# Reordered first loads, an identity load on ScalarE's queue, and eleven products of zeros ahead of the first fold

## The chip, the cores and the metric

The kernel runs on one core of a Trainium2 chip. A core has TensorE (PE: matrix products; the load of the stationary operand is listed apart as PEld), VectorE (DVE), ScalarE (ACT), GpSimd (POOL) and SyncE (SP). SP computes nothing here; it issues transfers between the chip's memory (HBM) and the core's working memory (SBUF). ScalarE and GpSimd can issue transfers too. Products land in PSUM, from which VectorE and ScalarE read. The metric is the time of one execution in device microseconds, as the median of several runs.

## The reference

The input x has 2048 rows of 512 numbers. Each row is normalized (`xn`, mean 0, variance 1), and two branches follow:

```python
xn = layernorm(x)
q, k, v = split(xn @ wqkv)                 # 32 heads of 16 numbers
pq, pk = q @ w_phi[h], k @ w_phi[h]        # a 16x16 matrix for each head
phi = concat(softmax(p), softmax(-p))      # of pq and of pk
o = phi_q (phi_k^T v) / (phi_q phi_k^T 1)  # linear attention
s = o @ wo
h = relu(xn @ W_gate) * (xn @ W_up)        # 1376 hidden numbers
g = silu(h @ W_down)
out = x + s * g
```

All inputs and the output are float32.

## The kernel before, in words

Rows of x are worked on in 16 tiles of 128 rows. Where a product needs more than one pass of reduced precision allows, each operand is split into a high part (a copy in the type float32r, by ScalarE) and a low part (the remainder, by VectorE or GpSimd); `mm3` then makes three products, low by high, high by low and high by high, in that order for each of the four slices of the contraction. So a product by a weight needs the weight's high and low part in SBUF.

The key and query weights aren't used as they come. `fold` (line 226) multiplies each block of 128x128 of a weight's row block with a block-diagonal matrix that holds `w_phi` (`bd_sb`, tile name cb), in plain float32, so that `xn` times the folded weight gives pq or pk at once. A fold of one row block `k` takes four float32 products into one PSUM tile, pfold; each of them stands in the trace as two matmul instructions. Calling what `fold` returns splits the result into the high and low part (wkh, wkl for the key rows, wqh, wql for the query rows). The key weight has four row blocks (`wk_raw[:, k, :]`, tile name wkT); "key row k" is short for row block k here, 128 partitions of 512 numbers, 256 KB.

A tile of x is normalized by `norm_vector` and `norm_vector_apply` (statistics on VectorE, a power on GpSimd, the scaling on VectorE). `turn` (line 304) transposes it on TensorE with the help of an identity matrix (`ident`, four instructions into the tile pxT) and writes the high part of the transposed tile into the tile XT (ScalarE); `lo_xt` (line 300) writes the low part (VectorE). `project` (line 346) multiplies the transposed tile with a weight by `mm3`: pk with the key weight, pv with the value weight, pq with the query weight.

The prologue (from line 829) issues all first loads on SP's queue, in the order in which the lines stand: x tile 0, the constants `bd_sb`, key row 0, the identity, key rows 1 to 3, x tile 1, query rows 0 and 1, value rows 0 and 1, query rows 2 and 3, x tile 2, value rows 2 and 3, x tiles 3 to 6. Then (from line 854) the work is written out by hand: statistics of tile 0; folds of key rows 0 and 1; scaling of tile 0; split of row 0; `turn(0)`; split of row 1; folds of key rows 2 and 3; `lo_xt` of tile 0; split of row 2; statistics of tile 1; split of row 3; scaling of tile 1; then pk of tile 0. The splits of the value rows (`wv_split`, GpSimd for the low part), the folds of the query rows and further tiles follow.

The main loop (line 904) goes over the 16 tiles of x; after it come two halves, each over the 22 blocks of the gate, up and down weights, with the attention's queries and the output between them. Every engine executes its instructions in the order in which the program emits them. `InOrder` and `Clock` (a planner) decide during emission where the pieces of secondary work go: `Clock.issued` charges every instruction with a cost in its own units, keeps for each engine the time at which it is reckoned free, takes a load as ready 8,000 units after its issue, and `due` lets a piece in when its engine is reckoned free soon enough. Its clock `now` is the time at which TensorE is reckoned free. A matmul on float32 operands is charged with

```python
if name == "matmul" and a[2].dtype == F32:
    cost = n * 3 + 460
```

where n is the number of columns. Tiles of SBUF come from pools: `u2` has 44 buffers of 2 KB in each partition, and `ps` is the pool of the eight PSUM tiles.

## Time and profile before

| what | value |
|---|---|
| runs shown, median (lowest to highest) | 586.2 us (585.45 to 586.35) |
| the profiled execution: its time, its span | 586.47 us, 584.7 us |
| PE, PEld busy | 572.5 us (98% of the span), 478.0 us (82%) |
| DVE, ACT, POOL busy | 395.4, 288.6, 390.2 us |
| mean transfer rate over the span | 236 GB/s |
| first product on PE | at 7.06 us |

The profile is one execution of the program, recorded by the hardware. Times in it count from the start of the span. A row of the timeline has the start, the length, the engine, the line (a helper records every operation, so all have line 52), the operation, the tiles written and read, and in brackets the idle time of the engine just before with what ended it. Rows with x16 stand for sixteen instructions in a run, and the matmuls are pipelined, so the last one's drain reaches into the next row. The granted clock is the share of full speed that the throttle of TensorE granted.

### The profile page before, as it was taken

Reading aid. Unit: us, or ns where it says so; the run is one execution under the profiler, and the core shown is the slowest. Engines: PE = TensorE matmul, PEld = TensorE weight load, DVE = VectorE, ACT = ScalarE, POOL = GpSimd, SP = SyncE. Lnnn points to the kernel's source line nnn. Section 1 sums busy time; section 2 is a strip of 40 time slices with the busy share of each in tenths; the row PEclk is TensorE's granted clock in tenths of the full one; section 3 lists DMA queues with packets and bytes.
Section 4 is the critical chain, followed back from the end, with each engine's and each line's share of the span. In section 5 each row is a group of like instructions: output and inputs, shape, how many; then the busy total and the mean of one; then the engine's idle time right before and its main releaser. Section 6 shows DMA issues by size and latency. Waiting matters only on the chain.

```text
span 584.7 us, 8483 instructions
## 1 busy us (share of the span) xinstructions
PE 572.5 (98%) x2764; PEld 478.0 (82%) x2764; DVE 395.4 (68%) x604; ACT 288.6 (49%) x529; POOL 390.2 (67%) x341
## 2 busy tenths in 40 slices
PE   4999999999999999999999999999999999999997
PEld 4788888888888888888888888888888888888886
DVE  2898765876647976787784532488788868673323
ACT  3798786864635356245434151153554545534510
POOL 0669987998866576997967342544457585775394
PEclk9999999999999999999999999999999999999999
DMA  8358897974698938978967999995576475669863
GB/s 289 112 150 223 221 307 233 265 222 126 164 279 272 347 95 261 301 263 293 283 215 226 319 389 398 315 390 193 130 266 170 137 227 169 183 206 275 254 176 113
DMA packets 82844, 138.26 MB, mean 236 GB/s; under 512 B 7664, under 2 KB 30576, under 8 KB 81904
## 3 DMA queue, kind: packets, MB, share of 16 engines
q1 hardware_dynamic: 79488, 125.66, 64.3%
q0 software_dynamic: 3312, 12.06, 10.8%
q8 instruction: 22, 0.36, 0.3%
q14 instruction: 22, 0.18, 0.1%
HBM read 77.14 MB, written 52.69 MB: 222 GB/s over the span
## 4 chain that ended last, share of the span: by engine, by line
PE 97%; DMA 1%; ACT 1%; DVE 1%; SPq 0%; issue 0%; POOL 0%; POOLq 0%
PE py L52 21%; PE pd L52 10%; PE pa L52 10%; PE pc L52 10%; PE pso L52 8%; PE pk L52 8%; PE pq L52 7%; PE pv L52 7%; PE pb L52 5%; PE pkv L52 3%; PE pnum L52 3%; PE ppT L52 2%; PE pxT L52 1%; PE pfold L52 1%; DMA wkT<-wkT 1%; PE pkb L52 0%
## 5 line engine op out<-in xcount | busy, mean ns | idle before, releaser
L52 PE MATMUL pa<-XT,wa 128*128 128x512 f32 x264 | 68.9, 393 | 0.0
L52 PE MATMUL py<-fdh,hl 128*128 128x512 f32 x176 | 68.8, 391 | 0.0
L52 PE MATMUL py<-fdh,hh 128*128 128x512 f32 x176 | 68.6, 390 | 0.0
L52 PE MATMUL py<-fdl,hh 128*128 128x512 f32 x176 | 68.5, 389 | 0.0
L52 POOL TENSOR_TENSOR hl<-e,hh 128x512 fp32r<-128x512 f32 x22 | 28.4, 1292 | 56.5 <-ACT hh L52 56.2
L52 PEld LDWEIGHTS pa<-XT,wa 128*128 128x128 f32 x264 | 48.5, 188 | 9.4
L52 ACT ACTIVATE hh<-e 128x512 fp32r<-128x512 f32 x22 | 13.9, 632 | 72.1 <-DVE e L52 67.4
L52 POOL TENSOR_TENSOR phl<-ek,phl 128x1024 fp32r<-128x1024 f32 x15 | 36.1, 2403 | 17.9 <-ACT phl L52 17.9
L52 POOL TENSOR_TENSOR hl<-u,hh 128x512 fp32r<-128x512 f32 x22 | 28.5, 1296 | 27.1 <-ACT hh L52 24.8
L52 DVE TENSOR_TENSOR y<-py,y 128x512 f32<-128x512 f32 x40 | 27.5, 689 | 27.2 <-PE py L52 27.1
L52 POOL TENSOR_TENSOR y<-y,ys 128x512 f32<-128x512 f32 x24 | 31.1, 1297 | 17.0 <-ACT ys L52 17.0
L52 PEld LDWEIGHTS py<-fdh,hh 128*128 128x128 f32 x176 | 33.0, 188 | 7.0
L52 PEld LDWEIGHTS py<-fdl,hh 128*128 128x128 f32 x176 | 33.0, 188 | 6.7
L52 PEld LDWEIGHTS py<-fdh,hl 128*128 128x128 f32 x176 | 33.1, 188 | 6.7
L52 POOL TENSOR_TENSOR ez<-eq,zB 128x1024 f32<-128x1024 f32 x16 | 38.4, 2405 | 0.0
L52 DVE TENSOR_TENSOR pTl<-ppT,pTh 128x512 fp32r<-128x512 f32 x32 | 22.1, 690 | 23.1 <-ACT pTh L52 22.7
L52 PE MATMUL pd<-XT,wd 128*128 128x512 f32 x132 | 34.9, 395 | 0.0
L52 PE MATMUL pd<-XT,wc 128*128 128x512 f32 x132 | 34.5, 392 | 0.0
L52 PE MATMUL pb<-XT,wb 128*128 128x512 f32 x132 | 34.5, 393 | 0.0
L52 PE MATMUL pc<-XT,wb 128*128 128x512 f32 x132 | 34.3, 391 | 0.0
L52 POOL TENSOR_TENSOR ol<-of,oh 128x1024 fp32r<-128x1024 f32 x8 | 19.4, 2431 | 22.2 <-ACT oh L52 15.3
L52 PE MATMUL pc<-XT,wc 128*128 128x512 f32 x132 | 34.1, 391 | 0.0
(163 smaller groups left out, 1632.8 us busy)
## 6 DMA issues: line engine op xcount, KB each, us to landing
zacc<-ek POOLq DMA_DIRECT2D x15, 512.0 KB, 5.2
xts<-XT SPq DMA_DIRECT2D x4, 1792.0 KB, 11.3
XT<-xts SPq DMA_DIRECT2D x7, 1024.0 KB, 15.8
wa<-ws SPq DMA_DIRECT2D x26, 256.0 KB, 5.3
wb<-ws SPq DMA_DIRECT2D x26, 256.0 KB, 5.3
wc<-ws SPq DMA_DIRECT2D x26, 256.0 KB, 4.9
rawg<-wf SPq DMA_DIRECT2D x22, 256.0 KB, 3.9
ws<-wa SPq DMA_DIRECT2D x22, 256.0 KB, 3.9
```

What stands on the lines that cost most here:

```text
L52: return self.tc.keep_in_program_order(op(*a, **k))
```

## The change

The load of the identity moves from SP's queue to ScalarE's, directly behind the issue of x tile 0 in the program. On SP's queue now stand x tile 0, the constants, key row 0, key row 1, and key rows 2 and 3 in one transfer of 512 KB; the rest follows as before. After the loads, VectorE fills a tile of 128x128 with zeros (`idle`), and TensorE multiplies it with itself eleven times in float32, into a PSUM tile that nobody reads. `lo_xt` of tile 0 moves ahead of the split of key row 1.

```diff
     load_x(0)
+    nc.scalar.dma_start(ident, cst[:, KD, :])
     nc.sync.dma_start(bd_sb, cst[:, :KD, :])
-    for k in range(KD):
+    for k in (0, 1):
         nc.sync.dma_start(wk_raw[:, k, :], wkT[:, k, :])
-        if k == 0:
-            nc.sync.dma_start(ident, cst[:, KD, :])
+    nc.sync.dma_start(wk_raw[:, 2:4, :], wkT[:, 2:4, :])
     load_x(1)
...
     for n in range(3, 7):
         load_x(n)
+
+    idle = u2((P, P), "idle")
+    nc.vector.memset(idle, 0.0)
+    p = ps((P, P), name="pidle")
+    for _ in range(11):
+        nc.tensor.matmul(p, idle, idle, start=True, stop=True)
     mhalf = sb.tile([P, 1], F32, name="mhalf")
...
     folds[0]()
     px = turn(0, False)
+    lo_xt(*px)
     folds[1]()
     folds = [fold(WK, wk_raw[:, k, :], k) for k in range(2, KD)]
-    lo_xt(*px)
     folds[0]()
     norm_vector(1)
```

## The prediction, written before the result was known

> **What bounds the kernel now.** I read the page's head and chain first, to see which engine sets the end.

> ```profile
> span 584.7 us, 8483 instructions
> ...
> PE 97%; DMA 1%; ACT 1%; DVE 1%; SPq 0%; issue 0%; POOL 0%; POOLq 0%
> ```

> The chain that ended last is TensorE work for 97%. Then the waits of PE from 26 to 584 us (one row: in all, times, longest) and the last stretch of the busy time by stage (stretch, its length, PE busy, weight loads, VectorE, ScalarE, GpSimd, granted clock, DMA share, GB/s).

> ```profile
> PE pxT L52 <- DVE lr L52: 0.2, 1, 0.2
> ```

> ```profile
> 500.00:584.70 84.70, 81.14 (x386) 67.33 (x384) 37.12 (x55) 27.41 (x42) 52.83 (x37) 1.00 0.71 208
> ```

> From 26 us to the last product PE waits 0.2 us in all; the idle 3.6 us of the last stretch (84.70 less 81.14), for which no wait is listed, lie behind the last product. So whatever the start gives or takes moves the end by the same amount, and only the first 26 us are to be argued. PE's rows there in order of time (start, length, what, how many, idle before and what ended it):

> ```profile
> 7.06 3.75 PE L52 MATMUL pfold<-cb,wkT 128*128 128x128 f32 x16 [7.06 <-DMA wkT<-wkT]
> 10.60 1.05 PE L52 MATMUL pxT<-ident,xn 128*128 128x128 f32 x4
> 11.46 1.99 PE L52 MATMUL pfold<-cb,wkT 128*128 128x128 f32 x16
> 14.25 0.47 PE L52 MATMUL pk<-wkh,XT 128*128 128x512 f32 x1 [0.81 <-DVE XT L52]
> ...
> 16.64 0.39 PE L52 MATMUL pk<-wkl,XT 128*128 128x512 f32 x1
> ```

> PE idles 7.06 us until the first key row lands. Two folds (16 instructions: each float32 product counts as two) then take from 7.06 to 10.60, the four transposes to 11.46, the other two folds to 13.44 (11.46 + 1.99), and the projection pk waits 0.81 us for VectorE's low part of XT. The same operations at two times, PE alone (stretch, length, PE busy, granted clock, DMA share, GB/s):

> ```profile
> 7.06:10.60 3.54, 3.54 (x16) 1.00 0.99 362
> 10.60:11.46 0.86, 0.86 (x6) 1.00 1.04 429
> 11.46:13.44 1.98, 1.98 (x17) 1.00 1.02 410
> 17.10:18.88 1.78, 1.78 (x18) 1.00 0.59 219
> 18.88:19.32 0.44, 0.44 (x7) 1.00 0.03 9
> ```

> Sixteen fold instructions take 3.54 us first and 1.78 us later, four transposes 0.86 and then 0.44: half speed until 11.46, full speed afterwards. The granted clock reads 1.00 in both, so it doesn't show this; nor is it the DMA traffic, since the share is 1.02 in the third row, where the fold is already fast. I take it for a TensorE that starts slow and turns fast once it has been busy for a while, here 11.46 - 7.06 = 4.40 us.

> **The change, part by part.** First the loads. SP's issues; then, from the view of DMA issues, the time from issue to landing (last column, us): of the first, the second and the fourth key row, each in the stretch of its own issue, and of value rows (median of two), constants and identity.

> ```profile
> 1.18 0.42 SPq L52 DMA_DIRECT2D cb<-cst  x1
> 1.65 0.42 SPq L52 DMA_DIRECT2D wkT<-wkT  x1
> 2.12 0.43 SPq L52 DMA_DIRECT2D ident<-cst  x1
> 2.60 1.38 SPq L52 DMA_DIRECT2D wkT<-wkT  x3
> ...
> 4.97 0.58 SPq L52 DMA_DIRECT2D wvr<-wv  x1
> ...
> 7.95 0.53 SPq L52 DMA_DIRECT2D wvr<-wv  x1
> ```

> ```profile
> wkT<-wkT SPq DMA_DIRECT2D x1, 256.0 KB, 5.3
> ```

> ```profile
> wkT<-wkT SPq DMA_DIRECT2D x1, 256.0 KB, 5.2
> ```

> ```profile
> wkT<-wkT SPq DMA_DIRECT2D x1, 256.0 KB, 6.2
> ```

> ```profile
> wvr<-wv SPq DMA_DIRECT2D x2, 512.0 KB, 8.1
> cb<-cst SPq DMA_DIRECT2D x1, 256.0 KB, 2.9
> ident<-cst SPq DMA_DIRECT2D x1, 64.0 KB, 5.0
> ```

> The constants land at 1.18 + 2.9 = 4.08, the first key row at 1.65 + 5.3 = 6.95, the identity at 7.12, the second key row at 7.8, the fourth key row at 2.60 + 2 x 0.47 + 6.2 = 9.74.

> *Identity to ScalarE's queue.* SP loses one issue (0.47 us between issues) and everything behind it is issued that much sooner; but with 362 to 429 GB/s running from 7 us on (above), landings follow the bytes ahead, and ahead of the fourth key row these stay the same. ScalarE has only its table load at that time (below). If the issue stands behind the table load it comes at 0.75 + 1.28 = 2.03, about where SP has it today. Lands by 7.1, wanted at 8.84 (below): hidden by 1.7 us. Ahead of the first key row its 64 KB would delay that by 0.2 us (it lands 0.17 after the key row today); 0 to 0.2, I take 0, because the fourth key row decides below.

> [...]

> *Third and fourth key row in one transfer.* SP loses a further issue. Fold 2 can start only when both rows are there; taken at 9.74, the landing of the fourth row today. Bounds: 2.4 us sooner or later, the excess of the first key row's 5.3 over the constants' 2.9, the largest step between neighbours in these rows.

> *Zeros and the products.* VectorE's rows and ScalarE's, start and length:

> ```profile
> 0.82 0.06 DVE L52 MEMSET mhalf<- 128x1 f32 x1 [0.82 <-PEq L1155]
> 3.49 0.69 DVE L52 BATCH_NORM_STATS2 bs<-xt 128x6 f32<-128x512 f32 x1 [2.61 <-DMA xt<-x]
> ```

> ```profile
> 12.81 0.69 DVE L52 TENSOR_TENSOR wkl<-pfold,wkh 128x512 fp32r<-128x512 f32 x1 [2.35 <-ACT wkh L52]
> 13.42 0.68 DVE L52 TENSOR_TENSOR XT<-pxT,XT 128x512 fp32r<-128x512 f32 x1
> 14.02 0.68 DVE L52 TENSOR_TENSOR wkl<-pfold,wkh 128x512 fp32r<-128x512 f32 x1
> ...
> 15.62 0.68 DVE L52 TENSOR_TENSOR wkl<-pfold,wkh 128x512 fp32r<-128x512 f32 x1
> ```

> ```profile
> 0.75 1.28 ACT L52 ACT_TABLE_LOAD   x1 [0.75 <-PEq L1155]
> ...
> 11.70 0.60 ACT L52 ACTIVATE XT<-pxT 128x512 fp32r<-128x512 f32 x1 [1.96 <-PE pxT L52]
> ...
> 18.18 0.60 ACT L52 ACTIVATE wqh<-pfold 128x512 fp32r<-128x512 f32 x1 [3.06 <-PE pfold L52]
> ...
> 21.06 1.18 ACT L52 ACTIVATE wvh<-wvr 128x512 fp32r<-128x512 f32 x2
> ```

> A fill of 128x128 lies between the 0.06 us of 128x1 and the 0.69 of the 128x512 operation; 0.2 taken. VectorE has nothing else until 3.49, when the first tile is there, so the fill is hidden, as is mhalf behind it. The products start near 1.1 and are 22 instructions at 3.54/16 = 0.221: 4.87 us, ending near 5.97 (5.7 if the speed turns after 4.40, at 5.5). That is 1.0 us before the key row: nothing is delayed. Without that cover each product costs 0.44 us of the end. They leave PE at full speed for the folds, as I take it: the gap to the key row is 1.1 us, and after today's gap of 0.81 us the rows from 14.25 on are fast. Bounds of this effect: nothing, or 1.76 (3.54 - 1.78) plus 0.42 (0.86 - 0.44).

> *XT's low part ahead of the second key row's.* Same operations; XT leaves VectorE 0.6 sooner against the rows beside it. That takes the 0.81 wait.

> **The sum.** Folds 0 and 1: 7.06 + 1.78 = 8.84 (the second key row is there since 7.8). Transposes to 9.28. Then PE waits for the merged key rows, which are late next: 9.74 plus the 0.11 between landing and first product today (6.95, 7.06) is 9.85. Folds 2 and 3: 11.63. XT's high part follows the transposes by 0.24 (11.46, 11.70): 9.5, ready 10.1, low part 10.8: not late. So pk starts at 11.63 instead of 14.25: 2.62 us. Of the 2.99 on offer (1.76 + 0.42 + 0.81) the wait for key rows eats the rest.

> Does it hold behind pk? Its tenth product is the one that wants the fourth low key row, 16.64 - 14.25 = 2.39 after the start, so at 14.02. Fold 2 is through at 9.85 + 0.89, its high part 0.24 + 0.60 later, so the third low row starts at 11.6, the fourth 1.60 behind it (14.02 to 15.62), done at 13.9: just in time, at worst 0.2 lost. Value rows 0 and 1 land at 4.97 + 8.1 = 13.1 and hold ScalarE for 1.15 us, to 14.3; its next piece, wqh, comes at 18.18 - 2.62 = 15.56: covered by 1.3. Value rows 2 and 3 land at 7.95 + 8.1 = 16.05, wanted at 21.06 - 2.62 = 18.44: covered by 2.4. So the whole 2.62 reaches the end.

> The profiled execution took 586.47 us, 0.27 above the median 586.2 of the runs shown. 586.47 - 2.62 = 583.85, or 583.6 against the median.

> **Rivals.**
> 1. *Landings come sooner (0.13).* Without the identity in its queue, the first key row might take the constants' 2.9: everything 2.4 sooner, the fourth row at 7.34. Then the products' end, 5.97, decides: folds to 7.75, transposes to 8.19, folds to 9.97, pk 4.28 sooner, less some 0.25 for the fourth low key row: 4.0 us, 582.2. For: 2.4 us between neighbours are odd. Against: the second and fourth rows took 5.2 and 6.2 as well.
> 2. *The speed does not turn (0.17).* The products occupy 4.9 us and today's turn took 4.40: 0.5 in hand, from one execution. If it fails, folds and transposes run as today to 13.44, and pk starts there because XT's low part is out at 12.30 + 0.68: 0.81 us, 585.4, no change that can be measured.
>  [...]
> 3. *Landings come later (0.07).* Two queues at once cost a second step of 2.4: fourth row at 12.14, pk at 14.03, 0.22 us, 586.0.
> 4. *The written order changes; slower (0.05).* The planner reckons each float32 product of this size as 3 x 128 + 460 = 844 units, 9,284 for eleven, and orders the main loop by its clock. Against: the loads are reckoned ready at 8,200, so today's first fold is reckoned from 8,400 on; all engines' reckoned times start from the tensor time, so all move by some 1,500 alike and differences stay. If not, pieces placed too early would make PE wait in the loop. Price: a wait of 0.25 us, as pv has for GpSimd now (below), once in each of the 22 blocks of F: 5.5 us, 589.1. It decides from some 15 such waits on (2.62 + 1.17 over 0.25).

> ```profile
> PE pv L52 <- POOL wvl L52: 0.5, 2, 0.3
> ```

> **How the numbers follow.** My forecast 583.6 has 0.58; its own range is 583.0 to 584.5 (fill, key rows, 0.2 at the low row). 0.2% is 1.17 us, about what a measurement here can tell from no change. Faster: forecast and rival 1, 0.71. Same: rivals 2 and 3, 0.24. Slower: 0.05. The range takes in rivals 1 and 2: 581.9 to 585.6; left out are rivals 3 and 4 and the tails, under 0.2.

> **What would show it.** The rows of pidle from about 1.1 to 6; pfold's first sixteen in about 1.8 us, pxT in 0.44; a wait of pfold for wkT of about 0.5 near 9.3; pk's first row near 11.6 without a wait for XT; no new wait of PE behind 26 us; the same order of work there. Wrong: pfold's first sixteen still at 3.5 us, a first row landing far from 6.9, or a second engine's wait ahead of pk.

## The result, and the profile after

The changed kernel took 583.79 us (median of eight runs, 583.24 to 585.47) against 585.84 us (585.37 to 586.35) for the kernel before, measured beside it. The ratio is 0.9968, with a 95% interval from 0.9958 to 0.9979: faster by 2.05 us by the medians. The profiled execution took 583.24 us with a span of 581.5 us; it is the lowest of its eight, so it shows the change at its best.

PE's rows after, in order of time (start, length, what, how many, idle before and what ended it):

```profile
1.06 4.59 PE L52 MATMUL pidle<-idle 128*128 128x128 f32 x22 [1.06 <-DVE mhalf L52]
6.51 2.02 PE L52 MATMUL pfold<-cb,wkT 128*128 128x128 f32 x16 [0.86 <-DMA wkT<-wkT]
8.37 0.60 PE L52 MATMUL pxT<-ident,xn 128*128 128x128 f32 x4
8.96 2.05 PE L52 MATMUL pfold<-cb,wkT 128*128 128x128 f32 x16
10.77 0.47 PE L52 MATMUL pk<-wkh,XT 128*128 128x512 f32 x1
...
13.18 0.51 PE L52 MATMUL pk<-wkl,XT 128*128 128x512 f32 x1
13.52 0.39 PE L52 MATMUL pk<-wkh,XT 128*128 128x512 f32 x1
```

The products of zeros fill PE from 1.06 to 5.65 (1.06 + 4.59). The first two folds go from 6.51 to 8.37, 1.86 us instead of 3.54, the transposes follow, and pk starts at 10.77 instead of 14.25 without a wait for XT. The loads behind this: the first key row and the merged rows, each from the stretch of its own issue in the view of DMA issues (last column: us from issue to landing), with the identity from the first 20 us and its issue on ScalarE's queue.

```profile
wkT<-wkT SPq DMA_DIRECT2D x1, 256.0 KB, 4.7
```

```profile
wkT<-wkT SPq DMA_DIRECT2D x1, 512.0 KB, 6.3
...
ident<-cst ACTq DMA_DIRECT2D x1, 64.0 KB, 3.1
```

```profile
0.74 0.40 ACTq L52 DMA_DIRECT2D ident<-cst  x1
1.17 1.28 ACT L52 ACT_TABLE_LOAD   x1 [1.17 <-PEq L1161]
```

Issued at 1.66 and 2.60, the key rows land at 6.4 and 8.9. ScalarE issues the identity ahead of its table load, not behind it, and it is there at 3.8. PE's waits in the first 26 us, from the view of waits:

```profile
PE pidle L52 <- DVE mhalf L52: 1.1, 1, 1.1
PE pfold L52 <- DMA wkT<-wkT: 0.9, 1, 0.9
PE pv L52 <- POOL wvl L52: 0.5, 2, 0.3
PE pxT L52 <- DVE lr L52: 0.2, 1, 0.2
```

From 26 us to the end that view lists no wait of PE at all. With buffer numbers left out, each engine's instructions stand in the same order in the two traces but for what the diff names.

### The profile page after: what moved, and what is told of

It reads as the page before. It is cut to its first block, busy times and chain, and to the rows that moved or that the text cites. A ratio compares the mean times of both kernels' runs of the same rounds, so it can differ in the third digit from the quotient of the medians.

```text
span 581.5 us, 8525 instructions
## 1 busy us (share of the span) xinstructions
PE 575.2 (99%) x2786; PEld 480.2 (83%) x2786; DVE 395.6 (68%) x605; ACT 289.4 (50%) x529; POOL 390.1 (67%) x341
## 3 DMA queue, kind: packets, MB, share of 16 engines
q0 software_dynamic: 3312, 12.06, 10.8%
## 4 chain that ended last, share of the span: by engine, by line
PE 97%; DMA 1%; ACT 1%; DVE 1%; SPq 0%; issue 0%; POOL 0%; POOLq 0%
PE py L52 21%; PE pd L52 10%; PE pa L52 10%; PE pc L52 10%; PE pso L52 8%; PE pk L52 8%; PE pq L52 8%; PE pv L52 7%; PE pb L52 5%; PE pkv L52 3%; PE pnum L52 3%; PE ppT L52 2%; PE pxT L52 1%; PE pfold L52 1%; DMA wkT<-wkT 1%; PE pkb L52 0%
## 5 line engine op out<-in xcount | busy, mean ns | idle before, releaser
L52 PE MATMUL pa<-XT,wa 128*128 128x512 f32 x264 | 68.9, 393 | 0.0
L52 PE MATMUL py<-fdh,hl 128*128 128x512 f32 x176 | 68.8, 391 | 0.0
L52 PE MATMUL py<-fdh,hh 128*128 128x512 f32 x176 | 68.6, 390 | 0.0
L52 PE MATMUL py<-fdl,hh 128*128 128x512 f32 x176 | 68.5, 389 | 0.0
L52 POOL TENSOR_TENSOR hl<-e,hh 128x512 fp32r<-128x512 f32 x22 | 28.4, 1292 | 56.1 <-ACT hh L52 51.8
L52 PEld LDWEIGHTS pa<-XT,wa 128*128 128x128 f32 x264 | 48.5, 188 | 9.4
L52 ACT ACTIVATE hh<-e 128x512 fp32r<-128x512 f32 x22 | 13.9, 632 | 72.0 <-DVE e L52 65.0
L52 POOL TENSOR_TENSOR phl<-ek,phl 128x1024 fp32r<-128x1024 f32 x15 | 36.1, 2405 | 19.2 <-ACT phl L52 19.2
L52 POOL TENSOR_TENSOR hl<-u,hh 128x512 fp32r<-128x512 f32 x22 | 28.5, 1294 | 27.1 <-ACT hh L52 27.1
L52 DVE TENSOR_TENSOR y<-py,y 128x512 f32<-128x512 f32 x40 | 27.5, 689 | 27.2 <-PE py L52 27.1
L52 POOL TENSOR_TENSOR y<-y,ys 128x512 f32<-128x512 f32 x24 | 31.0, 1295 | 17.0 <-ACT ys L52 17.0
L52 PEld LDWEIGHTS py<-fdh,hh 128*128 128x128 f32 x176 | 33.0, 188 | 7.0
L52 PEld LDWEIGHTS py<-fdl,hh 128*128 128x128 f32 x176 | 33.1, 188 | 6.7
L52 PEld LDWEIGHTS py<-fdh,hl 128*128 128x128 f32 x176 | 33.0, 188 | 6.7
L52 POOL TENSOR_TENSOR ez<-eq,zB 128x1024 f32<-128x1024 f32 x16 | 38.5, 2408 | 0.0
L52 DVE TENSOR_TENSOR pTl<-ppT,pTh 128x512 fp32r<-128x512 f32 x32 | 22.1, 690 | 23.1 <-ACT pTh L52 22.7
L52 PE MATMUL pd<-XT,wd 128*128 128x512 f32 x132 | 35.0, 395 | 0.0
L52 POOL TENSOR_TENSOR ol<-of,oh 128x1024 fp32r<-128x1024 f32 x8 | 19.4, 2433 | 23.0 <-ACT oh L52 16.1
L52 PE MATMUL pd<-XT,wc 128*128 128x512 f32 x132 | 34.5, 392 | 0.0
L52 PE MATMUL pb<-XT,wb 128*128 128x512 f32 x132 | 34.5, 393 | 0.0
L52 PE MATMUL pc<-XT,wb 128*128 128x512 f32 x132 | 34.3, 391 | 0.0
L52 PE MATMUL pc<-XT,wc 128*128 128x512 f32 x132 | 34.1, 391 | 0.0
## 6 DMA issues: line engine op xcount, KB each, us to landing
zacc<-ek POOLq DMA_DIRECT2D x15, 512.0 KB, 5.2
wa<-ws SPq DMA_DIRECT2D x26, 256.0 KB, 5.3
wb<-ws SPq DMA_DIRECT2D x26, 256.0 KB, 5.2
wc<-ws SPq DMA_DIRECT2D x26, 256.0 KB, 5.3
rawg<-wf SPq DMA_DIRECT2D x22, 256.0 KB, 3.6
ws<-wa SPq DMA_DIRECT2D x22, 256.0 KB, 4.1
```

The lines of the kernel that those rows point to most:

```text
L52: return self.tc.keep_in_program_order(op(*a, **k))
```

## The experiments

All are variants of the two kernels above. Medians are of 5 to 12 runs; the kernel before took 586.09, 586.08 and 586.12 us beside the three groups (1 to 4, 5 to 8, 9 to 12).

| | edit | median us (lowest to highest) | ratio to before, interval | pk starts in the profile |
|---|---|---|---|---|
| 1 | before, products only | 584.27 (583.42 to 586.94) | 0.9981 (0.9968 to 0.9993) | 14.06 |
| 2 | changed, no products | 585.77 (584.57 to 586.59) | 0.9995 (0.9986 to 1.0004) | 13.12 |
| 3 | before, XT's low part first | 585.66 (584.04 to 586.42) | 0.9993 (0.9984 to 1.0002) | 13.74 |
| 4 | changed, again | 583.65 (583.56 to 584.13) | 0.9967 (0.9955 to 0.9979) | 11.12 |
| 5 | changed, 5 products | 585.06 (584.03 to 586.63) | 0.9987 (0.9978 to 0.9996) | 13.51 |
| 6 | changed, 14 products | 584.73 (583.69 to 584.94) | 0.9974 (0.9963 to 0.9984) | 12.11 |
| 7 | changed, 24 products | 586.33 (584.75 to 589.62) | 1.0015 (0.9998 to 1.0031) | 12.33 |
| 8 | changed, identity on SP | 584.03 (583.38 to 585.31) | 0.9967 (0.9955 to 0.9979) | 10.63 |
| 9 | first key row late, 11 products | 588.58 (588.02 to 589.18) | 1.0043 (1.0031 to 1.0055) | 16.20 |
| 10 | first key row late, 24 products | 587.30 (585.66 to 590.36) | 1.0019 (1.0007 to 1.0030) | 15.63 |
| 11 | changed, key rows 2 and 3 apart | 583.16 (583.01 to 584.18) | 0.9953 (0.9941 to 0.9964) | 10.40 |
| 12 | changed, 24 products of ones | 586.12 (584.62 to 587.68) | 1.0001 (0.9990 to 1.0011) | 13.17 |

### Which part carries the gain: 1 to 4

Theory A is the prediction's: the products bring TensorE to full speed, and the loads only set when the folds can start. Theory B: the gain comes from the loads and VectorE's order.

Experiment 1 adds to the kernel before only

```diff
+    idle = u2((P, P), "idle")
+    nc.vector.memset(idle, 0.0)
+    p = ps((P, P), name="pidle")
+    for _ in range(11):
+        nc.tensor.matmul(p, idle, idle, start=True, stop=True)
     mhalf = sb.tile([P, 1], F32, name="mhalf")
```

> The kernel before with the eleven products alone; loads and the place of XT's low part as before. Theory A (the products bring TensorE to full speed, the loads matter little): first two folds in 1.8 us from about 7.06, transposes in 0.44, third and fourth fold to about 11.0; XT's low part, still behind the second key row's, is ready near 11.9, so pk starts near 12.0 instead of 14.25: 2.25 us, 583.6 us against 585.84. Theory B (the gain comes from the loads and the order of VectorE): no change, 585.8, folds at 3.5 us or a wait that eats it. If every part counts: between 584 and 585.

The median fell by 1.82 us, to 584.27. So the products alone bring most of the gain, and B falls; but the 583.6 was missed, and three of the eleven runs took 586.0 to 586.9, as much as the kernel before. The profiled execution is one of them (586.26 us), and it shows something that neither theory had. PE's rows, and then PE by stretches of 3.41 us (stretch, length, PE busy, granted clock, DMA share, GB/s):

```profile
1.06 4.08 PE L52 MATMUL pidle<-idle 128*128 128x128 f32 x22 [1.06 <-DVE mhalf L52]
7.40 3.63 PE L52 MATMUL pfold<-cb,wkT 128*128 128x128 f32 x16 [2.26 <-DMA wkT<-wkT]
```

```profile
0.54:3.95 3.41, 2.89 (x13) 1.00 0.50 179
3.95:7.36 3.41, 1.19 (x11) 1.00 0.74 199
7.36:10.77 3.41, 3.37 (x16) 0.50 0.97 378
10.78:13.00 2.22, 2.22 (x22) 1.00 1.02 415
```

The products end at 5.14, early (4.08 us for the 22 instructions, against 4.59 in the changed kernel), because TensorE turned fast at 3.95. The key row landed late, and after 2.26 us without work the folds ran at half speed again, sixteen instructions in 3.63 us against 3.75 without any product. Here the granted clock does show it, 0.50 from 7.36 to 10.77: the speed was there and was taken away. The other two long runs, 586.02 and 586.94, read a mean granted clock of 1.000 and 0.999, against 0.997 for this one, so they did not lose a step in this way; what made them long isn't shown.

Experiment 2 takes the products and the fill out of the changed kernel:

```diff
-    idle = u2((P, P), "idle")
-    nc.vector.memset(idle, 0.0)
-    p = ps((P, P), name="pidle")
-    for _ in range(11):
-        nc.tensor.matmul(p, idle, idle, start=True, stop=True)
```

> The changed kernel without the eleven products and the fill of zeros; loads and XT's low part as changed. Theory A: first two folds at half speed (3.5 us) from the landing of the first key row at 6.4 to 6.9, transposes 0.86, full speed some 4.4 us after the first fold, pk at 12.8 (landing 6.4) to 13.4 (landing 6.9): 584.4 to 585.0 us. Theory B: 583.8, as the changed kernel.

It took 585.77 us, not to be told from the kernel before. Its pk starts at 13.12, within A's 12.8 to 13.4, but some of this is lost at once. The eleventh product of pk is the one that reads the fourth low key row (the prediction counts it as the tenth). The eleventh and twelfth in experiment 2, and the twelfth in the kernel before:

```profile
15.78 0.50 PE L52 MATMUL pk<-wkl,XT 128*128 128x512 f32 x1
16.12 0.40 PE L52 MATMUL pk<-wkh,XT 128*128 128x512 f32 x1
```

```profile
16.87 0.39 PE L52 MATMUL pk<-wkh,XT 128*128 128x512 f32 x1
```

The twelfth product starts 16.12 - 13.12 = 3.00 after the first, where the kernel before takes 16.87 - 14.25 = 2.62: 0.38 us of the 1.13 are lost to the fourth low key row, which VectorE now makes just too late. The spans, 584.0 and 584.7, differ by the 0.7 that are left. The remaining distance from the expected 584.4 to 585.0 to the median of 585.77 has no row to it.

Experiment 3 moves only the low part of XT in the kernel before:

```diff
     px = turn(0, False)
+    lo_xt(*px)
     folds[1]()
     folds = [fold(WK, wk_raw[:, k, :], k) for k in range(2, KD)]
-    lo_xt(*px)
```

> The kernel before with the low part of XT ahead of the second key row's split alone. Both theories: the wait of 0.81 us of pk for XT goes, folds stay at half speed until about 11.4: 585.0 us. If the fourth low key row or another wait takes its place: 585.4 to 585.8.

It took 585.66 us, within the 585.4 to 585.8 of the case that another wait takes the old one's place, and its interval takes in no change. In its profile the first fold starts at 6.82, and pk has no wait for XT:

```profile
11.22 2.77 PE L52 MATMUL pfold<-cb,wkT 128*128 128x128 f32 x16
13.74 0.47 PE L52 MATMUL pk<-wkh,XT 128*128 128x512 f32 x1
...
16.45 0.39 PE L52 MATMUL pk<-wkh,XT 128*128 128x512 f32 x1
```

But it isn't the fourth low key row that takes most of it back: the twelfth product starts 16.45 - 13.74 = 2.71 after the first, 0.09 more than before. TensorE turned fast only at 12.92 in that execution, 6.1 us after its first fold, so that the third and fourth fold took 2.77 us instead of 1.99.

Experiment 4 is the changed kernel unaltered.

> The changed kernel once more, on this chip, for comparison and for a second record of when TensorE turns fast. Theory A with a turn at a fixed 3.8 to 4.4 us after the first product: turn between 4.9 and 5.5 us from the start of the span, times within 0.5 us of 583.8. [...]

583.65 us, with six runs between 583.56 and 584.13, and the turn at 5.04 (the 22 instructions of the products took 4.61 us). That is what a turn at a fixed time would give, but the later profiles speak against one (below). By medians the gain is 2.44 us here and 2.05 in the runs of the result; by medians of the same group the products alone have 1.82, and the other two parts together 0.32, which is not told from nothing.

### When TensorE turns fast and slow: 5 to 7, 9, 10 and 12

Experiments 5, 6 and 7 change the number of products in the changed kernel to 5, 14 and 24:

```diff
-    for _ in range(11):
+    for _ in range(5):
```

> The changed kernel with five products instead of eleven (about 1.06 to 3.2 us). If TensorE must be busy for some 4 us to turn fast: no turn before the first key row lands at 6.4, folds and transposes at half speed, as without products, 584.4 to 585.0 us. If a short stretch of work anywhere before is enough (the turn comes by time since the first product): folds in 1.8 us, 583.8 us.

> The changed kernel with fourteen products instead of eleven. With the turn near 4.9 us the products end near 6.0 us, still ahead of the first key row's 6.4 to 6.9: the profile of the folds unchanged, median 583.6 to 583.8 us. If some executions of the changed kernel lose time because the turn comes late, the longer run of products helps them: fewer times above 584.5 than with eleven. If the turn does not come by then (all cold) they end at 7.0 and cost up to 0.6 us.

> The changed kernel with 24 products: 18 instructions at 0.213 us to 4.9, 30 at 0.112 behind, end at 8.3 us, past the first key row. Theory A: TensorE is the path at once, the first fold starts at 8.3 instead of 6.5, pk at 12.3 instead of 10.8: 1.5 us more than the changed kernel, 585.3 us; each product past the landing costs 0.22 us. If the key rows' landing or VectorE bound pk and not TensorE: less than 0.7 us more, under 584.5.

Five products end at 3.6, and the first two folds of the profile go from 7.16 to 10.70, 3.54 us: no turn, as the first theory of that run has it. The median, 585.06, is just above its range.

Fourteen don't help: 584.73, where 583.6 to 583.8 was expected, though the interval overlaps that of the changed kernel. In the profile the cause isn't the products, which end at 6.55, drain included, with the first fold at 6.51, but the second key row: PE waits 1.33 us for it.

```profile
6.51 1.13 PE L52 MATMUL pfold<-cb,wkT 128*128 128x128 f32 x8
8.97 1.16 PE L52 MATMUL pfold<-cb,wkT 128*128 128x128 f32 x8 [1.33 <-DMA wkT<-wkT]
```

Twenty-four do in the profile what was expected: the folds queue behind them until 8.40, pk starts at 12.33 (12.3 expected), and that execution took 585.08 (585.3 expected).

```profile
1.06 7.50 PE L52 MATMUL pidle<-idle 128*128 128x128 f32 x48 [1.06 <-DVE mhalf L52]
8.40 1.95 PE L52 MATMUL pfold<-cb,wkT 128*128 128x128 f32 x16
```

But its other runs go up to 589.62, and the median of 586.33 is 1.0 above what was expected.

Experiments 9 and 10 make the gap in front of the first fold long on purpose. The loads of the changed kernel stand as below, with eleven and with 24 products:

```diff
-    for k in (0, 1):
-        nc.sync.dma_start(wk_raw[:, k, :], wkT[:, k, :])
+    nc.sync.dma_start(wk_raw[:, 1, :], wkT[:, 1, :])
     nc.sync.dma_start(wk_raw[:, 2:4, :], wkT[:, 2:4, :])
+    nc.sync.dma_start(wk_raw[:, 0, :], wkT[:, 0, :])
```

> The changed kernel with the first key row loaded behind the other three, so that it lands near 9 us and the eleven products (end near 5.6) leave a gap of some 3.4 us. Window theory (the record of the clock grants full or half speed for steps of 3.413 us, and takes full speed away after a step in which TensorE was busy a third of the time, as in the run with the products alone): folds at half speed again in most executions, pk at 15 to 17 us, 587.5 to 589.5 us. Theory that full speed, once there, stays over gaps of a few us: pk near 13.0, 585.5 us.

> The same late first key row with 24 products, which end near 8.3 us and leave a gap under 1 us. Window theory: folds at full speed, pk near 13.0, 585.5 us, 2 us or more under the same loads with eleven products. Other theory: no difference between the two.

With eleven, all five runs lie between 588.02 and 589.18, as the window theory has it. PE's first fold and PE by stretches:

```profile
9.55 3.75 PE L52 MATMUL pfold<-cb,wkT 128*128 128x128 f32 x16 [3.98 <-DMA wkT<-wkT]
```

```profile
1.43:4.84 3.41, 3.41 (x17) 1.00 0.79 237
4.84:8.25 3.41, 0.73 (x7) 1.00 0.98 318
8.26:11.67 3.41, 2.12 (x10) 0.50 1.02 374
11.67:15.08 3.41, 3.41 (x18) 0.50 1.03 411
15.09:17.00 1.91, 1.91 (x16) 1.00 1.05 388
```

With 24 and the same loads the median of 587.30 is 1.28 us below that with eleven, where 2 or more was expected; only the fastest two runs, 585.66 and 585.71, are near the expected 585.5.

The granted clock of the single runs says more than the medians. A step of 3.41 us at half speed takes 3.41 x 0.5 / 585 = 0.003 off the mean of an execution: the profile of experiment 1, with one such step, reads 0.997, that of experiment 9, with two, 0.993, and the profiles without one read 0.999 or 1.000. In experiment 9 all five runs read 0.993 or 0.997. In experiment 10 ten of twelve read 0.999 or 1.000, and only 590.36 and 589.23 read 0.996 and 0.997. So with 24 products, which reach up near the key row, ten of twelve executions kept the speed, and with eleven, a gap of 3.98 us in the profile, all five lost it. What made runs of up to 588.73 among the ten long is another thing, which isn't settled.

The profile fell on the slowest run, 590.36; there the products ended at 8.03, the key row came at 9.99, and the step in which this gap lay was 1.45 of 3.41 us busy:

```profile
3.92:7.33 3.41, 3.41 (x33) 1.00 0.79 239
7.33:10.74 3.41, 1.45 (x14) 1.00 1.03 350
10.75:14.16 3.41, 3.41 (x19) 0.50 1.02 412
```

The same table for the changed kernel (two rows), for fourteen products and for experiment 3:

```profile
1.60:5.01 3.41, 3.41 (x18) 1.00 0.94 259
5.01:8.42 3.41, 2.55 (x23) 1.00 0.97 317
```

```profile
5.49:8.90 3.41, 2.15 (x17) 1.00 1.00 326
```

```profile
6.10:9.51 3.41, 2.69 (x12) 1.00 0.91 326
9.51:12.92 3.41, 3.41 (x17) 1.00 1.03 419
```

The length of the steps is read where the clock reads 0.50: once 3.41 us in experiment 1 (10.77 - 7.36), twice that in experiment 9 (15.08 - 8.26 = 6.82). In the clock records of the profiles before and after, full speed lasts 573.439 and 576.852 us, 3.413 apart. Laid back in such steps from a change in each profile, the rows agree with one reading, an estimate from these few steps: full speed came or went at the end of a step by how busy TensorE had been in it. While slow, a step of 2.69 us busy (79%, experiment 3) did not bring the turn, one of 2.89 (85%, experiment 1) did, as did one of 2.86 (84%) in the profile of experiment 10. While fast, steps of 2.55 (75%, the changed kernel) and 2.15 (63%, experiment 6) kept the speed, steps of 1.45 (43%, experiment 10), 1.19 (35%, experiment 1) and 0.73 (21%, experiment 9) lost it. Where the steps lie differs from execution to execution: in the ten profiles with at least eleven products from 1.06 us on, the turn came between 3.9 and 6.8 us.

The gaps without work that began in the steps that lost the speed were 2.26 us (experiment 1), 1.96 us (experiment 10) and 3.98 us (experiment 9).

Experiment 12 fills the tile of the 24 products with ones:

```diff
-    nc.vector.memset(idle, 0.0)
+    nc.vector.memset(idle, 1.0)
```

> The changed kernel with 24 products of ones instead of zeros. If the long times of 24 products of zeros (up to 589.6) come from the data: all times between 584.7 and 586.5, median 585.3. If not: times spread to 588 and more as with zeros, median near 586.3; the executions above 588 then show a granted clock of 0.996 or 0.997.

The times spread with ones too, from 584.62 to 587.68, with a median of 586.12, so the data alone isn't the reason for the spread. They don't reach 588, though, and none of the twelve runs reads a clock below 0.999, while with zeros three of twelve do (588.95, 589.16 and 589.62 at 0.996 or 0.997, a step lost somewhere). Whether the data makes that difference can't be told from twelve runs each.

The profiled execution with ones (587.26 us) turned at 6.79 (the 48 instructions took 8.34 us, against 7.50 in experiment 7), so the 24 products held the first fold until 9.24 and pk started at 13.17. And it has a wait that the changed kernel doesn't have, near 103 us in the main loop. PE's wait, and ScalarE's row ahead of it:

```profile
102.61 0.47 PE L52 MATMUL pk<-wkh,a 128*128 128x512 f32 x1 [0.71 <-DVE ek L52]
```

```profile
97.36 0.42 ACT L52 ACTIVATE wa<-rawg 128x256 fp32r<-128x256 f32 x1 [5.40 <-DMA rawg<-wf]
```

A load of gate weights came so late that ScalarE stood 5.40 us, VectorE behind it, and PE 0.71 us behind that. The profile of experiment 10 has the same wait with 1.52 us. The written order is the same in all these kernels; what makes that load late in some executions isn't settled.

### The loads: 8 and 11

Experiment 8 puts the identity back on SP's queue:

```diff
     load_x(0)
-    nc.scalar.dma_start(ident, cst[:, KD, :])
     nc.sync.dma_start(bd_sb, cst[:, :KD, :])
     for k in (0, 1):
         nc.sync.dma_start(wk_raw[:, k, :], wkT[:, k, :])
+        if k == 0:
+            nc.sync.dma_start(ident, cst[:, KD, :])
```

> The changed kernel with the identity's load back on SP's queue behind the first key row. If the identity's place decides when the key rows land: first key row near 6.9 again and the merged rows near 9.7, pk 0.5 to 0.8 us later, 584.3 to 584.6 us. If not: the landing moves from execution to execution anyway, 583.8 us within 0.3.

584.03 us, ratio 0.9967 as for experiment 4, with the first fold at 6.63 and pk at 10.63: the identity's queue makes no difference that can be measured.

Experiment 11 loads key rows 2 and 3 apart:

```diff
-    for k in (0, 1):
+    for k in range(KD):
         nc.sync.dma_start(wk_raw[:, k, :], wkT[:, k, :])
-    nc.sync.dma_start(wk_raw[:, 2:4, :], wkT[:, 2:4, :])
```

> The changed kernel with key rows 2 and 3 in transfers of their own. If the merged transfer holds up the third fold (it waited 0.15 to 0.25 us in the profiles of the changed kernel): that wait goes, 583.5 us. If the landing of the last key row alone counts: 583.8 us, no difference.

583.16 us, and in its profile the folds and transposes run without a wait for a key row:

```profile
6.15 2.27 PE L52 MATMUL pfold<-cb,wkT 128*128 128x128 f32 x16
8.26 0.60 PE L52 MATMUL pxT<-ident,xn 128*128 128x128 f32 x4
8.69 1.95 PE L52 MATMUL pfold<-cb,wkT 128*128 128x128 f32 x16
10.40 0.48 PE L52 MATMUL pk<-wkh,XT 128*128 128x512 f32 x1
```

It is the lowest median here, but its interval (0.9941 to 0.9964) overlaps those of the changed kernel, so that it beats it isn't shown.

## Why the prediction was right

583.6 us was predicted, 583.79 measured, inside the range, and the likeliest case is the one that came. As a ratio the forecast is 583.6 / 586.2 = 0.9956, just past the interval's edge of 0.9958: the gain was put too large, 2.62 us against 2.05. That the two times agree to 0.2 us is in part luck. The kernel before ran 0.36 us below the 586.2 from which the forecast was taken, and the profiled execution, 0.61 better than its forecast of 583.85, is 0.55 below the median of its runs.

- *The start moves the end.* pk starts 3.48 us sooner in the profile, 0.13 of it is gone by the twelfth product of pk (13.52 - 10.77 = 2.75, against 2.62 before), and span and time are 3.2 shorter. Right; what takes the remaining 0.15 isn't known.
- *Products and full speed.* The products began at 1.06 (1.1 predicted) and ended at 5.65 (5.7 to 5.97); the folds took 1.86 us (1.78). Experiment 1 alone gives 1.82 us. Right, and the turn came 3.95 us after the first product.
- *XT's low part.* The wait of 0.81 us went. But alone it is worth 0.43 us by medians, within the uncertainty of its run. The next wait is for the fourth low key row, at the eleventh product of pk and not the tenth; the prediction had it at 0.2 at worst, and it cost 0.13 in the changed kernel, 0.09 in experiment 3 and 0.38 in experiment 2.
- *Landings.* The largest miss among the terms of the sum: the merged key rows were taken at 9.74 and landed at 8.9, the first at 6.95 and landed at 6.4. That is the step that made pk start 0.86 us ahead of the predicted 11.63 in the profiled execution; the wait for the merged rows, forecast at 0.57 (9.28 to 9.85), was some 0.15. In the other profiles with eleven or fourteen products and the first key row in its place among the changed loads, pk starts at 10.4 to 12.1. Rival 1, landings 2.4 us sooner, came true by a quarter to a third; its reason, the identity's place, fell with experiment 8. Nor are the changed loads as a whole shown to be the reason: with the same loads the first fold starts at 7.12 and 7.16 in the profiles of experiments 2 and 5, later than in the kernel before.
- *Rival 2, the speed does not turn.* This one was only half seen. The turn came ahead of the folds in every profile with eleven products but that of experiment 11, where it came half a microsecond into them (sixteen instructions in 2.27 us). It did not come after a set time of work, as the 4.40 us were read, but between 2.9 and 5.7 us after the first product in the ten profiles, which agrees with the end of a step of 3.41 us. What the prediction missed as well is that the speed can be lost again in the gap before the key row, which it held safe by comparison with a gap of 0.81 us. Experiments 1 (a gap of 2.26 us) and 9 (3.98 us) show it. The eight runs of the result all read a clock of 0.999 or 1.000, the 584.77 and 585.47 among them, so none of them lost a step. A turn that comes late leaves no mark in that mean (the profile of the kernel before reads 1.000, with two folds in 3.54 us), so a late turn and late landings stay open as the reasons for these two.
- *Rival 4, the written order.* It did not change. Rival 3 did not show either.

## What to carry to other kernels

Filler products were worth their place here (1.82 us by medians in experiment 1), where the first real product came at half speed and every later one is on the path; take enough of them that the stretch ahead of the first operand isn't mostly idle, since here steps of 3.41 us that were 43%, 35% and 21% busy took the speed away again and one 63% busy kept it. Past that landing further products hold the first real one up (13 more took 7.50 - 4.59 = 2.91 us and moved the first fold from 6.51 to 8.40), and the landing itself moves: under the same loads the first fold started between 6.51 and 7.16, where no product stood in its way. More than eleven were no better here: 14 took 584.73 and 24 took 586.33, against 583.65 and 583.79. When a wait is removed ahead of a saturated engine, look up the next operand of the same chain: here the fourth low key row took back part of what the XT move gave.
